# A fused attention and MLP block: inputs loaded on two queues, segment 0 projected in token halves, and a new instruction list

## The chip, the cores and the metric

The kernel runs on one core of one Trainium2 chip. The metric is device microseconds of one execution; the lower the better. The engines are PE (matrix multiply), ACT (ScalarE), DVE (VectorE), POOL (GpSimd) and SP (SyncE, which here only issues transfers). PE writes its results to eight banks of PSUM, from which ACT and DVE read.

## What is computed

The reference has two parts, each with a residual, on one sequence of 2048 tokens of width 640 in bf16.

```
h  = x + A(layernorm(x))          # attention with a memory, 32 heads of 20, 4 segments of 512 tokens
h2 = h + B(layernorm(h))          # silu(x @ w1) @ w2, with 1728 hidden columns

# A, for segment s of each head, phi(t) = t+1 where t>0, else exp(t):
p     = softmax(q_s k_s^T * 20**-0.5, causal)
a_dot = p v_s
a_mem = (phi(q_s) M) / (phi(q_s) z + 1e-6)
o     = g * a_mem + (1-g) * a_dot          # g = sigmoid(beta) per head
M    += phi(k_s)^T v_s ;  z += sum phi(k_s)
# then o @ wo
```

In segment 0 the memory is empty, so only softmax attention is left there.

## The kernel before, in words

The program is a list of named tasks. Each task is declared with the engines it may run on, what it reads and writes, and its buffers from pools; the order in which tasks are emitted, the engine of a task that may run on several, and the slot of every buffer are written out by hand in `ORDER` (L359). An entry such as `qe010y/A:0` would mean: this task, on ACT (D is DVE, G is POOL, S is SP), slot 0. Each engine takes its own tasks strictly in that order; a tracker (L43) adds the semaphore waits, so a task that waits holds up everything behind it on its engine. Transfers are entries of the list too and take a place on the queue of the engine that issues them.

Tasks of a segment s, with the lines of their instructions:

- `x0`, `x4` and so on load tokens, 128 to a block (L567); `w_q`, `w_k`, `w_wv`, `w_wo`, `w_w1_*`, `w_w2_*` load weights (L570). wq and wk land in raw form in the space of `sT` and are copied (`re_wq0` to `re_wk4`, L682 on ACT, L684 on DVE) into `wqr` and `wkr`, where four heads stand 32 rows apart and the 12 rows between take parts of other heads.
- layer norm: `n1_st` (L711, L714 on DVE), `n1_ra` and `n1_rb` (L720 and L725 on POOL: variance plus epsilon, then the power -0.5), `n1_ap` (L732). In segment 0 the result is transposed by PE (`n1_tp`, L741) and copied out by ACT (`n1_te`, L750); later by a transposing transfer (`n1_tr`, L756).
- `v` (L783) and its copy `ve` (L793, L794); the projections of Q and K `pr` (L817), five chunks c each, and their copies `qe` (L825 on ACT, L826 on DVE) into `QK`. `vt` (L857, twelve transfers of SP) gathers the parts of other heads from `QK` into `QKV`, so that 32 heads make eight groups of four: five in `QK`, three in `QKV`.
- the memory's features `ex` (L832), `pha` (L839), `phb` (L845), and M's update `kt`, `mz`, `ma`, `mb` (L1050 to L1094).
- per group, scores `qk` (L893), which fill four PSUM banks at once; their exps `e` (two of 1024 columns, L904 on ACT); the causal mask `mk` (L915 on POOL); the product with V, `av` (L936); its scaled copy `oe` (L949 on ACT, L951 on DVE); a transposing matmul with the memory's share, `tn` (L965, L969); the normalisation `nm` and `ad` (L982 to L1010). There are 168 exps. In segment 0 each group comes in two halves of queries: `x` (the first 256 tokens, 384 columns of scores per head) and `y`.
- `ot`, `wo`, `rs` (L1111 to L1127): output projection and residual; layer norm again; `h1` (L1153, 13 blocks of 128 hidden columns, and L1148, the tail of 64 columns, two tiles of 64 side by side in the array), `th` (tanh on ACT, L1162), `s` (L1168 on DVE), `h2` (L1195), `o` (L1208) and the store `out` (L1213). In segment 0 h1 is done in two halves of the tokens.
- `fill` (L604) are matmuls on zeros, put in by the list where PE would have nothing to do.

The tasks of segment s+1's projections, segment s's attention and segment s-1's MLP are interleaved in the list. At the end only PE's MLP work of the last segments is left.

At the start, x0, x1, wv, wq, wk, beta and the rest are issued by SP in that order, x2 and x3 by ACT. `QK`, `QKV`, `xT` and `hT` exist once each. All other transfers are SP's.

Of the kernel before, what the change touches and what calls it, by code (L numbers as in the profile page):

```python
# [6 lines left out]
ALU = mybir.AluOpType  # L7
# [340 lines left out]
SPLIT0 = ()  # L348
# [10 lines left out]
zpad:0 vpad0 iota x3:4 x1:3 x0:7 x2:5 sel w_wv:0 warm:0 vpad1 w_q:0 w_k halfc epsc beta x4:0,1,2,6 n1_st0:1 w_wo:0  # L359
w_w2_4 n1_st1:6 n1_ra0 w_w1_0:0 n1_rb0 n1_ap0:0 n1_ra1 n1_st2:2 fill30:0 n1_tp0:4 n1_rb1 n1_te0/A:0 n1_st3:0 n1_ra2  # L360
epsg0 n1_rb2 fill8:1 v00:0 mt1 n1_ap2:1 n1_ra3 n1_ap1:0 n1_rb3 n1_tp1:2 n1_tp2:6 mt2 n1_ap3:2 n1_te1/A re_wq1/D:0
n1_tp3:4 n1_te2/A re_wq4/D v01:2 ve00/D:1 n1_te3/A re_wq2/A pr010:6 re_wk0/A:0 re_wk1/D ve01/D pr011:7 qe010/D:0
re_wk3/D re_wk4/A lsc0 lsc1 re_wq0/D pr001:0 re_wk2/D qe011/A qk1x0:4 qe001/D:0 pr000:1 e1x2:5 n1_st6:0 e1x0 pr021:0
re_wq3/D qe000/A n1_ra6 mk1x_0 lsc2 n1_st7:4 ex001:0 qk0x0:4 n1_rb6 pr020:2 e0x2:0 mt3 mk1x_256 qe021/D:0 e0x0 lsc3
pr041:3 n1_st5:5 qe020/A vt00:0 n1_st4:7 qk2x0:4 n1_ra5 qe041/A:0 mk0x_0 pr031:1 zf0 vt09 vt06 e2x2:2 n1_rb5 mk0x_256
pr030:0 e2x0 n1_ap5:2 pha041:1 x8:8,9,10,11 qe031/A:0 mk2x_0 vt03 qk0yb0:4 qe030/D av1x:3 e0yb0:1 pr040:2 mk2x_256
n1_ra7 pha001:0 e0yb2 oe1x/D:0 av0x:3 qe040/D mk0yb_0 qk1yb0:4 oe0x/A:1 av2x:0 e1yb0:3 tn1x:1 v03:2 pha021:2 nm1x:3,0
e1yb2 mk0yb_256 phb001 n1_ap6:1 oe2x/A:0 mk1yb_0 qk3x0:4 ve03/D v02:0 n1_tr5:0 vt011 vt07 e3x2:4 vt04 n1_rb7 n1_st9:1
e3x0 ex021:2 ve02/D vt05 vt010 qk4x0:4 mk3x_0 n1_ra4 tn0x:2 e4x0:6 nm0x:0 vt01 mk3x_256 e4x2 n1_st8:6 fill7:3 qk0ya0:0
mta1 vt02 av3x:4 e0ya0:5 mk4x_0 vt08 oe3x/D:1 n1_st10:0 mk4x_256 e0ya2 fill6:5 qk1ya0:4 n1_tr6 v11:0 n1_rb4 e1ya0:0  # L370
n1_st11:3 n1_ra10 mta3 kt00:1 n1_ra8 e1ya2 av4x:2 ve11/D:0 tn2x:3 n1_ra11 phb021 qk5x0:4 n1_ap4:3 fill10:0 v12:0 e5x2:2
n1_ap7:1 n1_tr4 oe4x/D:0 e5x0 nm2x:1 ex011:2 n1_tr7 ve12/D qk6x0:4 mk5x_0 tn4x:2 e6x0:4 av0y:3 nm4x:0 mk5x_256 tn3x:0
e6x2 oe0y/D:0 kt02:0 n1_rb11 av5x:1 ex041:1 n1_ap11:3 qk7x0:4 mk6x_0 v10:2 nm3x:1 w_w2_5 e7x2:6 oe5x/D:1 mta2 mtb3 e7x0
mk6x_256 w_w1_1 w_w1_4 ve10/D qk2ya0:4 mk7x_0 v13:0 e2ya2:5 n1_ra9 mk7x_256 mk1yb_256 e2ya0 tn0y:2 av7x:3 ve13/D n1_rb8
oe7x/A:0 qk2yb0:4 nm0y:1 tn7x:0 e2yb0:1 av6x:1 nm7x:2 tn5x:2 av1y:3 e2yb2 oe6x/D:1 nm5x:3 tn6x:0 oe1y/A:0 qk3ya0:4
mk2yb_0 nm6x:0 e3ya0:2 n1_rb10 ot1:0 mk2yb_256 pha011:0 phb011 e3ya2 tn1y:2 pr101:1 mz02:0 qe101/D:0 av2y:3 ot0 ma02/A:3
qk3yb0:4 oe2y/D:1 mz00:1 e3yb2:0 phb041 pr100:3 ma00/D:0 kt01:1 nm1y:1 e3yb0 tn2y:2 zf1 qe100/D qk4ya0:4 mk3yb_0 kt04:0
wo1:0 e4ya0:6 nm2y:2 mk3yb_256 mtb1 e4ya2 w_w2_2 av3y:3 rs1 w_w1_3 ex031:0 qk4yb0:4 oe3y/D:0 w_w1_2 wo0:0 e4yb2:5
n2_st1:5 w_w2_1 e4yb0 epsg1 tn3y:2 ex101:1 n2_ra1 rs0 mm5 qk5ya0:4 pr140:3 n2_rb1 mk4yb_0 n2_st0:2 e5ya2:0 e5ya0 pr121:0
n2_ap1:0 n2_ra0 nm3y:0 qe140/A:0 mt0 n2_rb0 n2_tr1:0 qk5yb0:4 pr141:1 mta0 e5yb2:3 n2_ap0:2 mk4yb_256 n2_tr0 e5yb0 mtb0  # L380
pha031:1 phb031 av4y:2 mm6 qk6ya0:4 mm4 qe121/D:0 ex140:2 mk5yb_0 pr111:3 e6ya2:6 mk5yb_256 e6ya0 pr120:0 qe111/D:0
qe141/D ex121:0 qk6yb0:4 pha101:2 av5y:3 e6yb0:4 oe4y/D:0 h1_0_7_0:1 qe120/D e6yb2 h1_0_0_0:2 oe5y/D:1 th0_7_0:1 mk6yb_0
# [78 lines left out]
def build(nc, es, A_x, A_wq, A_wk, A_wv, A_wo, A_beta, B_x, B_w1, B_w2, out):  # L461
# [102 lines left out]
    def load_x(b0, n, prio, bw=2.1, kind="plain", engs=(SP,)):  # L564
        s0 = b0 % 12
        dma(f"x{b0}", [], [(X[b], [0]) for b in range(b0, b0 + n)],
            lambda e: e.dma_start(out=x_tok[:, s0:s0 + n, :], in_=xv[:, b0:b0 + n, :]), prio, bw, kind, engs=engs)  # L567
# [701 lines left out]
```

## Time and profile before

| | |
|---|---|
| median of 3 runs | 305.44 us (304.98 to 305.56) |
| the profiled execution: span from its first to its last instruction | 303.6 us |
| median less that span | 1.84 us |
| busy time of PE, ACT, DVE, POOL | 294.4, 226.6, 214.4, 141.7 us |
| first V matmul, first exp, start of the last exps | 9.03, 16.72, 240.89 us |
| end of the last matmul | 301.3 us |
| ACT busy in 16.7 to 37.7, 37.7 to 191, 191 to 242 us | 19.49, 142.74, 42.58 us |
| granted PE clock in every slice | 1.0 of full |

The profiler's own time of an execution is its span; the median includes what lies around it, and the table gives the difference. A line of a timeline reads: start, duration of the group, engine, line of the kernel, operation, output and input tile, shape, number of instructions, and in square brackets the idle time before it and who ended it. The line's duration runs from the first start to the last end; matmuls are pipelined, so that the next group starts before that end. A line of the table by stage gives the busy time of each engine in it with its instructions in parentheses, then the granted PE clock, the share of the 16 DMA engines that was busy, and the GB/s moved.

### The profile page before, as it was taken

The numbers are of one execution on the slowest core, as the hardware profiler recorded it, in microseconds if no ns is written. First come the engines' busy times: TensorE is split into PE (matmuls) and PEld (weight loads), VectorE is DVE, ScalarE is ACT, GpSimd is POOL, SyncE is SP. The second block draws the span as 40 slices with busy tenths as digits, with TensorE's granted clock in tenths as the row PEclk, the third lists the DMA queues.
The fourth block names the chain that finished last, engine by engine and source line by source line (L and its number), as shares of the span: only waits on it lengthen the run. The fifth ranks groups of instructions, "written<-read, shape, count | busy, mean of one in ns | idle before, by whom it ended". The sixth has DMA issues, their size and how long they took to land.

```text
span 303.6 us, 7334 instructions
## 1 busy us (share of the span) xinstructions
PE 294.4 (97%) x2934; PEld 167.9 (55%) x2934; DVE 214.4 (71%) x492; ACT 226.6 (75%) x321; POOL 141.7 (47%) x280
## 2 busy tenths in 40 slices
PE   6999989999999999999999999999999999999996
PEld 5634545466565455566643545556564466764565
DVE  4888967877868866958588975858847494835623
ACT  3689988999999999899889989968779951004500
POOL 3346574532875856546847317564564730400000
PEclk9999999999999999999999999999999999999999
DMA  6938375843544130063551300043241006221003
GB/s 211 363 104 159 69 153 87 272 37 77 166 87 75 39 42 2 2 122 69 106 154 42 67 19 0 2 89 69 56 97 36 2 0 89 43 66 66 0 3 107
DMA packets 48721, 24.65 MB, mean 81 GB/s; under 512 B 39152, under 2 KB 47600, under 8 KB 48688
## 3 DMA queue, kind: packets, MB, share of 16 engines
q1 hardware_dynamic: 48400, 23.86, 34.6%
q8 instruction: 23, 0.38, 0.5%
q10 hardware_dynamic: 288, 0.33, 0.4%
q14 instruction: 10, 0.08, 0.1%
HBM read 10.41 MB, written 2.62 MB: 43 GB/s over the span
## 4 chain that ended last, share of the span: by engine, by line
PE 72%; ACT 12%; DVE 7%; DMA 4%; SPq 2%; issue 1%; POOL 0%; ACTq 0%
PE ps_all L1195 17%; PE ps_all L1153 13%; PE ps_all L817 13%; ACT PT L904 8%; PE ps_all L893 7%; PE ps_all L1119 6%; PE ps_all L783 5%; PE ps_all L936 5%; DVE sT L1168 3%; DMA wv_sb<-in_A_wv_dram 2%; ACT th L1162 2%; PE ps_all L965 2%; PE ps_all L1058 2%; DMA x_tok<-in_A_x_dram 1%; PE ps_all L969 1%
## 5 line engine op out<-in xcount | busy, mean ns | idle before, releaser
L904 ACT ACTIVATE PT<-ps_all 128x1024 bf16<-128x1024 f32 (+1 forms) x168 | 156.3, 985 | 16.9 <-PE ps_all L893 15.9
L915 POOL TENSOR_SCALAR_AFFINE_SELECT PT<-PT 128x512 bf16<-128x512 bf16 x128 | 81.5, 650 | 52.8 <-ACT PT L904 51.5
L1195 PE MATMUL ps_all<-w_sb,sT 128*128 128x320 bf16 (+2 forms) x462 | 64.8, 295 | 0.1
L1153 PE MATMUL ps_all<-hT,w_sb 128*128 128x512 bf16 (+1 forms) x325 | 62.5, 337 | 0.5 <-DVE sT L1168 0.4
L1162 ACT ACTIVATE th<-ps_all 128x512 f32<-128x512 f32 (+2 forms) x70 | 34.0, 505 | 35.1 <-PE ps_all L1153 24.6
L1168 DVE SCALAR_TENSOR_TENSOR sT<-th,ps_all 128x512 bf16<-128x512 f32 (+2 forms) x70 | 37.6, 558 | 23.8 <-ACT th L1162 23.2
L1195 PEld LDWEIGHTS ps_all<-w_sb,sT 128*128 128x128 bf16 x462 | 43.2, 98 | 18.5 <-issue 1.9
L1153 PEld LDWEIGHTS ps_all<-hT,w_sb 128*128 128x128 bf16 x325 | 29.8, 98 | 25.4 <-issue 2.1
L1010 POOL TENSOR_TENSOR otok<-on 128x320 bf16<-128x320 bf16 x24 | 19.2, 804 | 23.7 <-DVE on L1002 23.6
L711 DVE BATCH_NORM_STATS2 stt<-x_tok 128x6 f32<-128x320 bf16 x64 | 27.8, 476 | 3.4 <-DMA x_tok<-in_A_x_dram 3.2
L1208 DVE SCALAR_TENSOR_TENSOR x_tok<-ps_all,x_tok 128x640 bf16<-128x640 f32 (+3 forms) x18 | 13.3, 748 | 19.0 <-PE ps_all L1195 18.9
L720 POOL TENSOR_TENSOR rst<-mvt,eps_c 128x1 f32<-128x1 f32 x32 | 7.1, 223 | 40.4 <-DVE mvt L714 36.0
L817 PE MATMUL ps_all<-xT,wqr 128*128 128x512 bf16 x100 | 25.0, 381 | 0.0
L783 PE MATMUL ps_all<-wv_sb,xT 128*128 128x320 bf16 x160 | 24.4, 300 | 0.4 <-DMA wv_sb<-in_A_wv_dram 0.3
L817 PE MATMUL ps_all<-xT,wkr 128*128 128x512 bf16 x100 | 24.8, 380 | 0.0
L1119 PE MATMUL ps_all<-wo_sb,oT 128*128 128x320 bf16 x160 | 24.1, 299 | 0.4 <-DVE rd L996 0.2
L936 PE MATMUL ps_all<-PT,Vx 128*32 128x256 bf16 (+3 forms) x576 | 24.4, 287 | 0.0
L893 PE MATMUL ps_all<-QK 20*128 20x256 bf16 (+3 forms) x360 | 20.5, 286 | 1.0 <-ACT PT L904 0.7
L1002 DVE TENSOR_TENSOR on<-ps_all,rd 128x640 bf16<-128x640 f32 x24 | 19.8, 824 | 1.9 <-POOL otok L1010 1.1
L826 DVE CAST QK<-ps_all 128x512 bf16<-128x512 f32 x25 | 16.9, 684 | 5.1 <-PE ps_all L817 5.0
L1119 PEld LDWEIGHTS ps_all<-wo_sb,oT 128*128 128x128 bf16 x160 | 14.8, 97 | 8.1 <-issue 2.8
L783 PEld LDWEIGHTS ps_all<-wv_sb,xT 128*128 128x128 bf16 x160 | 14.7, 98 | 7.9 <-issue 1.5
(71 smaller groups left out, 329.4 us busy)
## 6 DMA issues: line engine op xcount, KB each, us to landing
out_dram<-x_tok SPq DMA_DIRECT2D x15, 160.0 KB, 1.9
w_sb<-in_B_w_dram SPq DMA_DIRECT2D x5, 432.0 KB, 4.5
x_tok<-in_A_x_dram SPq DMA_DIRECT2D x3, 640.0 KB, 5.3
w_sb<-in_B_w_dram SPq DMA_DIRECT2D x3, 480.0 KB, 3.8
QKV<-QK SPq DMA_DIRECT2D x16, 72.0 KB
wv_sb<-in_A_wv_dram SPq DMA_DIRECT2D x1, 800.0 KB, 7.2
sT<-in_A_wq_dram SPq DMA_DIRECT2D x1, 800.0 KB, 8.9
sT<-in_A_wk_dram SPq DMA_DIRECT2D x1, 800.0 KB, 10.6
```

The costliest lines, as they stand in the source:

```text
L711: T.add(DV, lambda e, hh=hh: e.bn_stats(out=stt[:, s, 6 * hh:6 * hh + 6], in_=xb[:, 320 * hh:320 * hh + 320]), reads=R((xa, xsub)), writes ...
L783: fns.append(lambda e, c=c, hh=hh: e.matmul(bank(ps, hh)[:, 0:320], lhsT=xT[:, c, 128 * i:128 * i + 128], rhs=wv_sb[:, c, 320 * hh:320 * h ...
L817: fns = [lambda e, kc=kc: e.matmul(bank(ps)[:, lo:hi], lhsT=wt[:, kc, c, :], rhs=xT[:, kc, lo:hi], start=(kc == 0), stop=(kc == NC - 1)) f ...
L893: fns.append(lambda e, j=j, o=o, r=r, q0=q0, q1=q1, qa=qa, ka=ka: e.matmul(ps_all[:, o:o + q1 - q0], lhsT=ka[32 * r:32 * r + DH, 128 * j:1 ...
L904: T.add(AC, lambda e: e.activation(out=pt[:, pta.slot, q0:q0 + 2, 0:width], in_=sc3[:, b0:b0 + 2, 0:width], func=ACT.Exp, scale=SCALE), re ...
L915: T.add(PO, lambda e: e.affine_select(out=v, in_=v, pattern=[[0, 4], [1, 128]], compare_op=ALU.is_ge, fill=0.0, base=0, channel_multiplier ...
L936: fns.append(lambda e, j=j, r=r, h=h, pa=pa, pt=pt, co=co, q0=q0, ji=ji: e.matmul(bank(po)[32 * r:32 * r + 32, q0:hi], lhsT=Vx[:, vx.slot, ...
L1119: fns.append(lambda e, c=c, hh=hh: e.matmul(bank(ps, hh)[:, 0:320], lhsT=oT[:, c, 128 * i:128 * i + 128], rhs=wo_sb[:, c, 320 * hh:320 * h ...
L1153: fns = [lambda e, c=c: e.matmul(bank(ps)[:, lo:hi], lhsT=w1_sb[:, c, 128 * f:128 * f + 128], rhs=hT[:, c, lo:hi], start=(c == 0), stop=(c ...
L1162: T.add(AC, lambda e: e.activation(out=th[:, tha.slot, lo:hi], in_=bank(ps)[:, lo:hi], func=ACT.Tanh, scale=0.5), reads=R((ps, [0])), writ ...
L1168: T.add(DV, lambda e: e.scalar_tensor_tensor(out=sT[:, f, lo:hi], in0=th[:, tha.slot, lo:hi], scalar=1.0, in1=bank(ps)[:, lo:hi], op0=ALU. ...
L1195: fns.append(lambda e, f=f, t0=t0, fr=fr, hh=hh, n=n: e.matmul(bank(pa, hh)[:, 0:n], lhsT=sT[:, f, t0:t0 + 128], rhs=w2_sb[:, fr, c0 + 320 ...
```

## The change

- The first loads: SP issues x0, wq, wv's first three fifths, beta, x4, wo and w1; ACT issues x1, x2, x3, wk, the rest of wv, and x8.
- Segment 0's projections of Q and K are done in halves of 256 tokens (`pr..x`, `pr..y`): 20 groups of five 256-column matmuls for ten of five 512-column ones. The first scores need only the first half. V is projected after them.
- Segment 0's Q and K stand in the space of w2 (`QZ`, `QZV`) and its transposed x in `hT`; `QK`, `QKV` and `xT` are left to the later segments. w2's four large loads therefore wait for the scores of segment 0.
- Tasks may be issued elsewhere: `vt`, w2's loads, `x8` and the stores by SP or ACT; the addition of epsilon by DVE or POOL. By the new list ACT issues 22 transfers (2 before): five at the very start, x8, eight `vt`, two w2 loads and six stores. 15 of the 20 half copies of segment 0's Q and K are on ACT.
- The tail of h1 is computed in four tiles of 32 columns by 128 or 256 tokens each, for two of 64: 20 matmuls for ten.
- `ORDER` is new as a whole. It holds one `fill` (37 matmuls, at the start); before there were 61 in five places.

Instruction counts of the two programs, where they differ: PE 2936 and 3012 (matmuls of projections, tails and fill); on ACT 512-column copies of Q and K 15 and 5, 256-column ones 0 and 15, copies of V 5 and 10, `oe` of 512 columns 13 and 9, of 256 columns 4 and 2, rearranging copies of wq and wk 7 and 2; DVE takes what ACT lost and the reverse. `th`, `ex` and the exps are the same in number.

The core of the diff:

```diff
-SPLIT0 = ()
+SPLIT0 = tuple((c, w) for c in range(5) for w in range(2))
...
+    w2_flat = w2_sb[:, :, :].rearrange("p f e -> p (f e)")
+    QZ = w2_flat[:, 0:10 * L].rearrange("p (c w t) -> p c w t", c=5, w=2)
+    QZV = w2_flat[:, 10 * L:16 * L].rearrange("p (c w t) -> p c w t", c=3, w=2)
...
-    load_x(1, 1, -99, 2.33, "fix", (SP,))
-    load_w("wv", wv_sb[:, :, :], cw(A_wv), -98, 4.96, [(W["wv"], [0])], "fix", (SP,))
+    load_x(1, 1, -100, 2.33, "fix", (AC,))
...
+    load_w("q", wraw[:, 0, :, :], cw(A_wq), -99, 6.58, [(sT0, ["q"])], "fix", (SP,))
+    load_w("k", wraw[:, 1, :, :], cw(A_wk), -99, 8.51, [(sT0, ["k"])], "fix", (AC,))
+    load_w("wv0", wv_sb[:, 0:3, :], cw(A_wv[0:384, :]), -95, 4.96, [(W["wv"], [0])], "fix", (SP,))
+    load_w("wv1", wv_sb[:, 3:5, :], cw(A_wv[384:640, :]), -95, 4.96, [(W["wv"], [1])], "fix", (AC,))
...
+    def load_w2():
+        qk, va = segs[0]["qk"], (segs[0]["qv"], list(range(12)))
+        WA = {0: [(qk[0], WH), (qk[1], WH), (qk[2], WH[:2])], 1: [(qk[2], WH[2:]), (qk[3], WH), (qk[4], WH[:2])],
+              2: [(qk[4], WH), va], 3: [va]}
+        for k, (f0, f1) in enumerate(((0, 4), (4, 7), (7, 10), (10, 13))):
+            load_w(f"w2_{k}", w2_sb[:, f0:f1, :], cw(B_w2[128 * f0:128 * f1, :]), 2 + k, 0.45 * (f1 - f0),
+                   [(W["w2"], [k])] + WA[k], engs=(SP, AC))
...
+            if eng == DV:
+                T.add(DV, lambda e: e.tensor_scalar(out=rst[:, s, :], in0=mvt[:, s, 1:2], scalar1=EPS, scalar2=None,
+                                                    op0=ALU.add), reads=R((st, ["mv"])), writes=R((st, ["r"])))
...
-        xTa = G.alloc("xT")
+        xTa = G.alloc("xT" if s else "hT")
+        xT_ = xT if s else hT
...
+        QK_, QKV_ = (QZ, QZV) if s == 0 else (QK, QKV)
...
-            dma(f"vt{s}{n}", reads, [(qv, [n])], lambda e: e.dma_start(out=o, in_=i_), pr, 0.25, "sb", lane=lane_v[n % 3 > 0])
+            dma(f"vt{s}{n}", reads, [(qv, [n])], lambda e: e.dma_start(out=o, in_=i_), pr, 0.25, "sb", lane=lane_v[n % 3 > 0], engs=(SP, AC))
...
-                            bank(ps)[64 * k:64 * k + 64, lo:hi], lhsT=w1_sb[:, c, 128 * f:FF],
-                            rhs=hv[:, c, k, b0 // 2:b1 // 2, :], start=(c == 0), stop=(c == NC - 1),
-                            tile_position=(0, 64 * k)) for c in range(NC) for k in range(2)]
+                            bank(ps)[32 * k:32 * k + 32, lo:hi],
+                            lhsT=w1_sb[:, c, 128 * f + 32 * (k % 2):128 * f + 32 * (k % 2) + 32],
+                            rhs=hv[:, c, k // 2, b0 // 2:b1 // 2, :], start=(c == 0), stop=(c == NC - 1),
+                            tile_position=(0, 32 * k)) for c in range(NC) for k in range(4)]
...
-                    pr, 0.6, lane=lane_o)
+                    pr, 0.6, lane=lane_o, engs=(SP, AC))
```

The start of the new list, up to the first exps:

```
epsc:0 zpad mt0 iota vpad0 sel x1:3 n1_st1:6 mta0 mtb0 mm6 mm4 mt2 mm2 x0:7 x2:5 mta2 x3:4 mtb2 epsg0 mm7 mt1 mt3
w_k:0 w_wv1:0 n1_st0:1 n1_st2:2 halfc n1_r1/G n1_ap1:1 n1_r0/G n1_ap0:0 w_q mta3 n1_r2/G mm9 mtb3 n1_st3:0 w_wv0 beta
x4:0,1,2,6 re_wq2/D:0 re_wq0/D n1_ap2:3 warm:0 w_wo:0 mm11 mm8 w_w2_4 x8/A:8,9,10,11 re_wk0/D:0 w_w1_0:0 w_w1_3
n1_r3/G mta1 mm0 w_w1_1 re_wk2/D n1_ap3:2 re_wq1/D re_wk3/D re_wq3/D mtb1 mm1 fill37:0 mm3 w_w1_2 vpad1 w_w1_4 mm5
mm10 w_w2_5 n1_tp1:1 n1_te1/A:0 n1_tp0:6 n1_te0/A pr020x:5 re_wk1/A qe020x/A:0 pr000x:6 qe000x/A:0 n1_tp2:3 n1_te2/A
pr001x:2 qe001x/A pr011x:6 qe011x/A:0 zf0 re_wk4/D zf1 lsc0 lsc1 mzc4 mzc8 mzc11 mzc6 mzc5 mzc10 lsc2 re_wq4/D
n1_st4:7 mzc7 mzc9 n1_r4/G mzc3 mzc1 mzc2 mzc0 epsg1 n1_st7:4 n1_st6:5 n1_r6/G n1_r7/G n1_tp3:0 n1_te3/A pr010x:3
qe010x/A qk0x0:4 e0x2:0 e0x0
```

## The prediction

> **What bounds the kernel now.** I read the busy line first, then the chain of work that ended last, then the timelines of PE and ACT in the middle of the run.
>
> ```profile
> PE 294.4 (97%) x2934; PEld 167.9 (55%) x2934; DVE 214.4 (71%) x492; ACT 226.6 (75%) x321; POOL 141.7 (47%) x280
> ...
> PE 72%; ACT 12%; DVE 7%; DMA 4%; SPq 2%; issue 1%; POOL 0%; ACTq 0%
> ```
>
> A busy PE need not be a full one, so I compare starts with starts:
>
> ```profile
> 114.74 1.24 PE L817 MATMUL ps_all<-xT,wkr 128*128 128x512 bf16 x5
> 115.82 0.71 PE L1153 MATMUL ps_all<-hT,w_sb 128*128 128x256 bf16 x5
> 116.50 0.40 PE L893 MATMUL ps_all<-QKV 20*128 20x512 bf16 x4
> 116.83 1.25 PE L817 MATMUL ps_all<-xT,wkr 128*128 128x512 bf16 x5
> ```
>
> Each group starts before the one ahead has ended: five 512-column matmuls take 1.08 us start to start, a score group of four 0.33. Between them there is no hole, and from 45 us to the end I found none above 0.5. So PE is the bound. ACT comes next: by the busy times by stage it works 142.7 of the 153.3 us from 37.7 to 191. PE is idle 9.2 us in all (303.6 less 294.4): 1.1 before its first instruction, 1.2 and 0.35 before 9.03, 2.3 after its last one (301.3 to 303.6), and 4.2 elsewhere. Beside that stand filler matmuls on zeros: 38 before 9.03, and 23 later (some 2.6 us at 0.11 each). Useful work starts at 9.03 but for one transpose. That is all there is to win: about 8.6 us at the start, 6.8 in the middle.
>
> **Part 1, the loads and the start.** What must land before the first scores changes: x, wq and wk now go ahead of wv, on two queues. Before, by stage:
>
> ```profile
> 3.00:4.00 1.00, 1.00 (x7) 0.73 (x5) 0.00 (x0) 1.00 (x1) 0.00 (x0) 1.00 1.07 387
> 4.00:5.00 1.00, 1.00 (x9) 0.81 (x8) 0.22 (x1) 0.26 (x1) 0.00 (x0) 1.00 0.68 224
> ...
> 9.00:10.00 1.00, 0.97 (x8) 0.73 (x9) 0.96 (x4) 0.00 (x0) 0.86 (x4) 1.00 1.06 389
> ```
>
> The last column is GB/s: 387 while SP and ACT both have a queue filled, 224 to 323 from 4 to 8 us with SP alone, 350 to 390 from 8 us, still SP alone. wk landed at 2.79 + 10.6 = 13.4 us, when 3.70 MB had moved, though 3.04 MB stood in front of its end: landing lags by some 0.65 MB. In the new order wk ends as the fifth transfer of ACT's queue (1.28 MB); with an equal share for SP's that is 2.56 MB, with the lag 3.2. At 380 from 3 us on (0.26 MB moved by then) wk lands at 10.75; at the rates of before 12.0; with half the lag 9.9. I take 10.75, since the row with two queues is the 387.
>
> [...]
>
> From wk on: the rearranging copies on ACT (0.53 + 0.40, less overlap) end at 11.7. ACT then has, in its new order, four half evacuations and one more before the first exp (128x256 reads: 0.39 by the th row, 0.31 start to start), two transposed blocks (0.70 each, 0.6) and two small exps (0.22): 11.7 + 1.55 + 1.2 + 0.3 = 14.75, say 14.85. PE's pieces in between (0.55 per half projection, 0.33 scores) end earlier; its holes there are some 1.3 us, and after the hole of 1.2 before 7.36 the granted clock stayed at 1.0. x8, which ACT now issues before its first transposed block, meets an ACT that waits anyway. Before it was
>
> ```profile
> 16.72 1.51 ACT L904 ACTIVATE PT<-ps_all 128x768 bf16<-128x768 f32 x2 [0.77 <-PE ps_all L893]
> ```
>
> So ACT starts its exps 1.9 us sooner (1.2 later or 0.9 sooner at the ends). But what counts is PE. In segment 0, 15 half evacuations on ACT replace five whole ones. Counting by mean durations, ACT does 23.75 us between the starts of exp 1 and exp 19 (36 instructions, each overlapping the next by 0.08: 20.9), against 19.5 before, of which 1.5 idle. Exp 19 starts at 35.7 instead of 36.22. PE has done the same by then in both: 20 transposing matmuls (1.2), 5 V blocks (7.1), the projections (11.0; as 20 halves at 0.56, 11.2), 10 score groups (3.3), 4 or 5 AV groups (1.4), 24.2 us in all. So the start is worth **-0.5 us** (-1.5 to +0.8), halves included. Doing projections before wv costs PE what the sooner exps bring: before, V matmuls filled 9.03 to 13.
>
> **Part 2, w2's space for segment 0's Q and K, hT for its x.** No instruction is added; w2's four loads now wait for the scores of segment 0, two of them on ACT, ahead of exps whose scores PE computes after the ones waited for, so those waits are met when ACT comes to them. The last is issued soon after the scores of segment 0 end (63 us before), lands 3.8 us later by the issues' list, and h2 first needs it at 81: some 10 us of cover, and I cost it at nothing. Were it late, PE, which takes its groups in order, would stand still for as long. The gain, that segment 1's projections need not wait for QK, has no wait in the trace of before to remove: 0.
>
> **Part 3, copies moved between ACT and DVE.** From exp 19 to the last, ACT has 5.0 us less to do (203.6 against 208.6 by counts times mean rows: fewer QK and oTs evacuations, more Vx). PE waits in that stretch are 3.5 us in all, and 1.1 of filler; the ones I see are mostly of scores for ACT. ACT is not the bound there, so I take a quarter, **-1.2** (0 to -3.5). DVE gains some 5 us on 214 and nine additions to the variance; it has 89 us idle: 0.
>
> **Part 4, the tail of h1 in four tiles of 32 instead of two of 64.** Five tails; columns per tile are the same, matmuls double to 20.
>
> ```profile
> 192.79 0.74 PE L1148 MATMUL ps_all<-hT,w_sb 128*64 128x256 bf16 x10
> 193.46 0.39 PE L893 MATMUL ps_all<-QK 20*128 20x512 bf16 x4
> ...
> 39.13 0.57 PE L936 MATMUL ps_all<-PT,Vx 128*32 128x256 bf16 x16
> 39.66 0.25 PE L969 MATMUL ps_all<-ident,oTs 128*128 128x84 bf16 x2
> ```
>
> A whole tail takes 0.67 now, a half one 0.40 (123.70 to 124.10). The nearest row with 32-wide tiles is AV: 16 matmuls in 0.53, 33 ns each however few their columns. 20 make 0.68: 2 x 0.28 + 3 x 0.02 to 0.07, **+0.8** (0 to 1.4).
>
> **Part 5, transfers issued by ACT amid its work.** Between its first and its last exp ACT now issues eleven: eight of the virtual-head copies, two w2 loads, one store. Before it issued none there, only two at the start:
>
> ```profile
> 0.80 0.87 ACTq L567 DMA_DIRECT2D x_tok<-in_A_x_dram  x2
> 1.70 1.28 ACT L585 ACT_TABLE_LOAD   x1 [1.70 <-PEq L1254]
> ...
> L857 SPq DMA_DIRECT2D QKV<-QK x12: 624/682/897, 21.3 to 32.2; - x12
> ```
>
> Each issue holds its queue: 0.43 there, and the table load begins only after them; 0.68 for a virtual-head copy on SP. Upper end: all of it delays the exps queued behind: 8 x 0.68 + 2 x 0.5 + 0.43 = 6.9 us, and PE, whose next scores need the PSUM banks that these exps read, waits with them. Lower end 0: ACT's rows overlap (two exps of 1.02 in 1.94), so the queue runs ahead of the engine. No row shows an issue behind a running exp; the nearest is the one above, with nothing in front. I take 0.25 each, nearer to hidden because an exp lasts 1.0 and the issue 0.7: **+2.75**. On SP nothing waits that the chain shows (2%), so relief there is 0.
>
> **Part 6, the new list's end.** PE work left after the last scores is 59.0 us of columns against 58.5, and h1 of segment 3 alternates its two th buffers somewhat better (before, 19 us for 14.6 of columns, with h2 matmuls filling most): 0.
>
> **Sum**: -0.5 - 1.2 + 0.8 + 2.75 = +1.85. The profiled span is 303.6; 1.84 us of the 305.44 median lie around it and stay. 303.6 + 1.84 + 1.85 = **307.3 us**.
>
> **Rivals.**
> - *Hidden issues, ACT relief in full* (faster). If the issues cost nothing, and PE's 3.5 us of waits and half of its 1.1 us of filler go: -0.5 - 4.0 + 0.8 = -3.7, rounded against late waits to -2.8: 302.6; with wk at 9.9, 301.7. For it: ACT's overlapping rows and its 5 us less. Against: PE's waits are few already, and some are for DVE. [...]
> - *Full price of the issues* (slower still): -0.5 + 0.8 + 6.9 = +7.2, 312.6. It decides from 0.1 us per issue on: there eleven issues outweigh the -0.9 of the other terms.
> - *No change*: the terms cancel at about 0.1 us per issue: 305.4.
> - *The change does not do what it says*: wk lands no sooner (12.0 us): 308.5, inside the range.
>
> **How the numbers follow.** Forecast (306.1 to 310) 0.43, full price 0.18, hidden 0.31, no change 0.08. The low end is 301.7, the high end 312.6. A measurement of this kernel tells about 0.2% (0.6 us) from no change. Faster 0.31, same 0.08, slower 0.61.
>
> **What would show it.** First exp at 14 to 16 us and exp 19 near 35.7 (part 1); L1148's successor starting 0.68 us after a tail; ACT's idle before an exp just behind an ACTq row of 0.25 (part 5; near 0 makes the hidden rival, 0.6 the full price); PE idle plus filler between 36 us and 240 us above 4.6 us. I would be wrong if PE's waits fall below 2 us there, or if the first exp comes after 17 us.

## The result, and the profile after

The changed kernel takes 309.48 us (median of four runs, 307.8 to 310.2) against 305.21 before (304.25 to 305.56): a ratio of 1.0137, 95% interval 1.0102 to 1.0172, some 4.2 us slower. One run of experiment 4 and one of the kernel before, with a mean granted clock of 0.69 and 0.85, are left out of all comparisons. The forecast was 307.3. The profiled run took 309.25 us, its span is 307.5 (before 303.6), and its last PE instruction ends at 305.03 (before 301.29): the 3.74 us to explain.

The page of the changed kernel, busy shares and chain:

```profile
PE 293.9 (96%) x3010; PEld 171.8 (56%) x3010; DVE 221.8 (72%) x513; ACT 224.4 (73%) x319; POOL 141.3 (46%) x271
...
PE 74%; ACT 9%; DVE 7%; DMA 6%; issue 1%; ACTq 1%; SPq 1%; DVEq 0%
```

PE is still the bound, but DMA has gone from 4 to 6% of the chain: by lines, wk's load holds 3% and the transposes of the attention output (oT) 2%. The busy line says nothing of what was lost, so I compared the starts of the same exps in both traces: exp 1 at 17.78 (before 16.72), exp 19 at 39.05 (36.22), exp 97 at 136.8 (135.0), exp 168 at 245.47 (241.81). So 2.83 us are lost by exp 19, 1.03 are won back by exp 97, 1.86 are lost behind it, and 0.08 after the last. Exp 19, before and then in the changed kernel:

```profile
36.22 1.51 ACT L904 ACTIVATE PT<-ps_all 128x768 bf16<-128x768 f32 x2 [0.54 <-PE ps_all L893]
```

```profile
39.05 1.51 ACT L925 ACTIVATE PT<-ps_all 128x768 bf16<-128x768 f32 x2
```

**The start.** ACT's timeline, then PE's, then the stages (the last three columns are the granted clock, the DMA share and GB/s):

```profile
13.02 0.83 ACT L692 ACTIVATE wkr<-sT 128x400 bf16<-128x400 bf16 x2 [3.48 <-DMA sT<-in_A_wk_dram]
...
17.78 1.51 ACT L925 ACTIVATE PT<-ps_all 128x768 bf16<-128x768 f32 x2
```

```profile
7.75 0.81 PE L759 MATMUL ps_all<-ident,xn_rot 128*128 128x128 bf16 x10 [1.13 <-DVE xn_rot L750]
10.00 1.71 PE L837 MATMUL ps_all<-hT,wqr 128*128 128x256 bf16 x10 [1.44 <-DVE wqr L694]
...
13.50 2.32 PE L837 MATMUL ps_all<-hT,wkr 128*128 128x256 bf16 x10 [1.25 <-DVE wkr L694]
```

```profile
8.00:10.00 2.00, 0.56 (x10) 0.35 (x7) 1.58 (x8) 1.30 (x2) 1.62 (x7) 1.00 0.60 175
...
12.00:14.00 2.00, 0.75 (x6) 0.39 (x4) 0.98 (x5) 0.98 (x3) 0.67 (x4) 0.50 1.07 377
14.00:16.00 2.00, 2.00 (x13) 1.45 (x12) 1.65 (x12) 1.41 (x5) 0.00 (x0) 0.50 1.07 364
```

wk lands at 13.0 us; ACT and PE wait for it. Between 6.6 and 13.5 PE has three holes above a microsecond, and from 10.6 to 17.5 us the granted clock is 0.50: the ten matmuls at 13.50 take 2.1 us start to start, at full clock 1.09 (experiment 10). By links, exp 19's delay of 2.83 is -0.36 (ACT's rearranging of wk begins at 13.02, before at 13.38), +1.42 (from there to exp 1: 4.76 against 3.34), +1.77 (exp 1 to exp 19: 21.27 against 19.50).

**The wait at 139.** PE, and SP's queue ahead of it:

```profile
141.06 1.53 PE L1140 MATMUL ps_all<-wo_sb,oT 128*128 128x320 bf16 x10 [1.90 <-DMA oT<-otok]
```

```profile
130.53 2.55 SPq L1132 DMA_TRANSPOSE oT<-otok  x2
134.41 1.33 SPq L877 DMA_DIRECT2D QKV<-QK  x2
135.78 3.58 SPq L1132 DMA_TRANSPOSE oT<-otok  x2
```

All four blocks' data were there by 130.5 (POOL's last addition to otok starts at 129.71 and takes 0.79). But SP takes its list in order: two transposes, then a virtual-head copy that waits for a projection until 134.4, and the other two transposes behind it. In the trace of before no hole of PE from 105 us on is above 0.4.

### The profile page after: what moved, and what is told of

It reads as the page before. It is cut to its first block, busy times and chain, and to the rows that moved or that the text cites. A ratio compares the mean times of both kernels' runs of the same rounds, so it can differ in the third digit from the quotient of the medians.

```text
span 307.5 us, 7509 instructions
## 1 busy us (share of the span) xinstructions
PE 293.9 (96%) x3010; PEld 171.8 (56%) x3010; DVE 221.8 (72%) x513; ACT 224.4 (73%) x319; POOL 141.3 (46%) x271
## 3 DMA queue, kind: packets, MB, share of 16 engines
HBM read 10.41 MB, written 2.62 MB: 42 GB/s over the span
## 4 chain that ended last, share of the span: by engine, by line
PE 74%; ACT 9%; DVE 7%; DMA 6%; issue 1%; ACTq 1%; SPq 1%; DVEq 0%
PE ps_all L1217 20%; PE ps_all L1175 15%; PE ps_all L837 11%; ACT PT L925 7%; PE ps_all L914 7%; PE ps_all L1140 6%; PE ps_all L957 5%; PE ps_all L802 5%; DMA sT<-in_A_wk_dram 3%; PE ps_all L986 2%; DMA oT<-otok 2%; PE ps_all L1079 1%; PE ps_all L990 1%; DMA w_sb<-w_sb 1%; DVE stt L728 1%; DVE oTs L972 1%
## 5 line engine op out<-in xcount | busy, mean ns | idle before, releaser
L925 ACT ACTIVATE PT<-ps_all 128x1024 bf16<-128x1024 f32 (+1 forms) x168 | 157.0, 986 | 14.4 <-PE ps_all L914 12.5
L936 POOL TENSOR_SCALAR_AFFINE_SELECT PT<-PT 128x512 bf16<-128x512 bf16 x128 | 82.6, 651 | 78.3 <-ACT PT L925 75.1
L1175 PE MATMUL ps_all<-hT,w_sb 128*128 128x512 bf16 (+1 forms) x325 | 63.2, 337 | 0.0
L1184 ACT ACTIVATE th<-ps_all 128x512 f32<-128x512 f32 (+2 forms) x70 | 34.6, 508 | 37.8 <-PE ps_all L1169 19.5
L1190 DVE SCALAR_TENSOR_TENSOR sT<-th,ps_all 128x512 bf16<-128x512 f32 (+2 forms) x70 | 38.4, 562 | 20.0 <-ACT th L1184 19.4
L957 PE MATMUL ps_all<-PT,Vx 128*32 128x256 bf16 (+3 forms) x576 | 23.5, 287 | 1.2 <-DVE rd L1003 0.8
L744 POOL TENSOR_TENSOR rst<-rst,eps_c 128x1 f32<-128x1 f32 x32 | 18.5, 577 | 11.4 <-DVE rst L738 9.6
L972 DVE TENSOR_SCALAR oTs<-ps_all,lsc 128x512 bf16<-128x512 f32 (+1 forms) x29 | 17.7, 617 | 4.8 <-PE ps_all L957 4.5
L750 DVE TENSOR_SCALAR xn_rot<-x_tok,mvt,rst 128x640 bf16<-128x640 bf16 x32 | 15.7, 498 | 5.2 <-POOL rst L744 5.2
L837 PE MATMUL ps_all<-xT,wqr 128*128 128x512 bf16 x75 | 18.7, 380 | 0.3 <-ACT PT L925 0.3
L837 PE MATMUL ps_all<-xT,wkr 128*128 128x512 bf16 x75 | 18.7, 380 | 0.1
L957 PEld LDWEIGHTS ps_all<-PT,Vx 128*32 128x32 bf16 x576 | 12.4, 96 | 10.8 <-issue 3.5
```

The lines of the kernel that those rows point to most:

```text
L837: fns = [lambda e, kc=kc: e.matmul(bank(ps)[:, lo:hi], lhsT=wt[:, kc, c, :], rhs=xT_[:, kc, lo:hi], start=(kc == 0), stop=(kc == NC - 1)) ...
L925: T.add(AC, lambda e: e.activation(out=pt[:, pta.slot, q0:q0 + 2, 0:width], in_=sc3[:, b0:b0 + 2, 0:width], func=ACT.Exp, scale=SCALE), re ...
L936: T.add(PO, lambda e: e.affine_select(out=v, in_=v, pattern=[[0, 4], [1, 128]], compare_op=ALU.is_ge, fill=0.0, base=0, channel_multiplier ...
L957: fns.append(lambda e, j=j, r=r, h=h, pa=pa, pt=pt, co=co, q0=q0, ji=ji: e.matmul(bank(po)[32 * r:32 * r + 32, q0:hi], lhsT=Vx[:, vx.slot, ...
L972: f = lambda e: e.tensor_scalar(out=o, in0=i_, scalar1=lsc[:, g:g + 1], scalar2=None, op0=ALU.mult)
L1175: fns = [lambda e, c=c: e.matmul(bank(ps)[:, lo:hi], lhsT=w1_sb[:, c, 128 * f:128 * f + 128], rhs=hT[:, c, lo:hi], start=(c == 0), stop=(c ...
```

## The experiments

Each experiment runs the changed kernel with the edit shown, but for the last but one. Ratios are to the kernel before on the same chip.

**1. Fillers in the start's holes.**

```diff
- fill37:0
+ fill44:0
- n1_tp0:6 n1_te0/A pr020x:5 ... n1_tp2:3 n1_te2/A pr001x:2
+ n1_tp0:6 n1_te0/A fill11:0 pr020x:5 ... fill4:0 n1_tp2:3 n1_te2/A fill11:0 pr001x:2
```

> The changed kernel with 33 more matmuls on zeros at the start (37 becomes 44, and 11, 4 and 11 in the three waits of PE between 8.5 and 13.5 us); no other instruction moves, and the waits for wq and wk stay as long as they were. Theory A (the start costs two things: PE waits, and in them the granted clock falls to 0.50 until 18 us, which makes 25 projection matmuls take 4.8 us in place of 2.75): the clock stays near 1.0, PE saves about 2, the first exp comes near 16 us in place of 17.8, and the time is 307.3 to 308 in place of 309.5. Theory B (the slow matmuls stand under the wait for wk and for ACT, so that the clock costs nothing): the clock is back at 1.0 and the time stays at 309.5 +-0.4. If the clock stays low even so, it doesn't hang on PE's holes.

307.15 us, 1.0069 (1.0043 to 1.0094); clock 1.00 through the profiled run. The time fits theory A, the trace does not: exp 1 is at 17.72. ACT met wk at 14.16 there, 1.1 later, and from wk to exp 1 it took 3.56 in place of 4.76. So the clock is worth 1.2 us behind wk, and the rest of the gain in this trace is the wait at 139, which did not come (the same two transposes, issued at 135.69, landed some 2 us sooner). The four traces with this order of transposes have the wait at 1.90 (the change), 2.19 (experiment 2), 0.82 (3) and nothing (1). So it differs from run to run, and both causes had to be taken apart.

**2. wk second on ACT's queue.**

```diff
- x1 ... x2 ... x3 ... w_k w_wv1      (ACT's queue; n1_st2 and n1_st3 right behind n1_st0)
+ x1 ... w_k x2 ... x3 ... w_wv1      (n1_st2, n1_st3, n1_ap2 behind re_wk0; n1_tp2 behind pr011x)
```

> The changed kernel with wk as the second transfer of ACT's queue, ahead of x2 and x3; the statistics and the transposes of blocks 2 and 3 go behind the first rearranging copies and the first four half projections. Theory A (wk's landing at 13.0 us, not the half projections, is why the first exp came 1.1 us later than before): 0.98 MB of ACT's queue end with wk in place of 1.31, so it lands at 8.5 to 11, PE's wait of 1.3 at 13.5 goes, the first exp comes at 14.5 to 16, and the time is 306.5 to 308. Theory B (what the queue gives first is paid back: x2 and x3 now land after 11 us, their transposes and the copies on ACT wait, and exp 7 comes no sooner than 24.5): 309 to 310.

311.26 us, 1.0199 (1.0177 to 1.0221). wk landed at 9.68, and it is slower than theory B even: ACT and PE stood waiting for blocks 2 and 3.

```profile
14.26 0.45 PE L759 MATMUL ps_all<-ident,xn_rot 128*128 128x128 bf16 x5 [2.42 <-DVE xn_rot L750]
```

In PE's list the transposes of blocks 2 and 3 stand ahead of the first scores, which need only blocks 0 and 1. Exp 1 came at 17.40, and the clock was 0.50 from 15.9 to 19.3 us and again from 43.2 to 46.6.

**3. ACT's transfers back on SP.**

```diff
- vt07/A vt011/A vt03/A vt15/A ... w_w2_0/A w_w2_2/A ... out6/A ...
+ vt07/S vt011/S vt03/S vt15/S ... w_w2_0/S w_w2_2/S ... out6/S ...
```

> The changed kernel with the 16 transfers that ACT issues behind its first exp (eight copies for the virtual heads, two loads of w2, six stores) issued by SP, in the same places of the list. Theory A (the issues lie under running exps, since ACT's sequencer takes them while its engine works): the time stays within 0.5 of 309.5, or grows by the waits that SP's longer queue makes for the transposes behind it. Theory B (the prediction's part 5, 0.25 us each for eleven of them): 306.7, 2.75 less. At the full 0.6 each it would be 303.

310.50 us, 1.0189 (1.0153 to 1.0225): not faster, theory A. From exp 19 to exp 168, where eight of the eleven issues lie, it takes 205.36 us, in the changed kernel 206.43; less each one's oT wait (0.82 and 1.90) that is 204.54 and 204.53. Eight issues at 0.25 would have made 2.0. The change's own trace shows why:

```profile
24.47 0.81 ACT L925 ACTIVATE PT<-ps_all 128x768 bf16<-128x768 f32 x1
24.55 1.49 ACTq L877 DMA_DIRECT2D w_sb<-w_sb  x1
25.17 0.81 ACT L925 ACTIVATE PT<-ps_all 128x768 bf16<-128x768 f32 x1
26.09 0.66 ACT L845 ACTIVATE w_sb<-ps_all 128x256 bf16<-128x256 f32 x2
```

An issue of 1.49 us (24.55 to 26.04) runs beside two exps: the one of 25.17 starts in the middle of the issue, and ACT is idle 0.11 behind it. Whether a longer issue would lie under exps as well, no run here shows. On the other side, SP alone needed 8.91 us for the twelve copies of segment 0 (23.69 to 32.6) where SP with ACT needed 6.79 (24.55 to 31.3), and PE then waited 1.81 for them at 34.86 (0.47 in the changed kernel); behind that wait the granted clock was 0.50 from 36.3 to 39.8.

**4. The two oT transposes ahead of the copies.**

```diff
- ot7 pha240:0 ... qe230/D vt210/S ... vt24/S ... ot4 mk16e_0 mk16e_256 ot5 ex240:2
+ ot7 ot4 ot5 pha240:0 ... qe230/D vt210/S ... vt24/S ... mk16e_0 mk16e_256 ex240:2
```

> The changed kernel with one move on SP's queue: the transposes of blocks 4 and 5 of the attention output go ahead of two copies for segment 2's virtual heads, which wait for a projection. Theory A (PE's wait of 1.9 us at 139 is SP's order: the copy waits to 134.4 and both transposes, whose data are there by 130.5, stand behind it): they are issued by 133, land by 136, the wait goes, and the time is 307.5 to 308. Theory B (PE runs into the next thing that is late, scores for ACT or the copies that now come 2.5 us later): 309 to 309.7.

307.96 us, 1.0080 (1.0053 to 1.0108): theory A by the time. The trace of this kernel is that of experiment 9.

**5. Experiments 1 and 4 together.**

> Both edits that gained, together: the 33 more fillers of fill_holes and the two transposes ahead of ot_ahead. In fill_holes' trace the first exp came when it did before (17.72, with wk landing 1.1 later, at 14.16), and the wait of 1.9 us at 139 was missing, so its 2.3 us may be partly that wait. Theory A (the two are separate, the half clock costs 1.2: first exp 4.76 us behind wk in the changed kernel, 3.56 with fillers): 306.4 to 307.1, that is 309.5 less 1.2 less 1.5. Theory B (the sums of the medians hold, 2.3 and 1.5): 305.7. Theory C (fillers do nothing but that the wait at 139 happened not to come): 308.0, as ot_ahead.

306.65 us, 1.0051 (1.0033 to 1.0069): theory A. wk at 12.52, exp 1 at 16.07 (3.55 later), clock 1.00, no wait at 139. It is the base of the next three and of experiment 10.

**6. beta behind x4.**

```diff
- w_wv0 beta x4:0,1,2,6
+ w_wv0 x4:0,1,2,6 beta       (its readers zf0, lsc0 and so on behind the third exp)
```

> ot_fill with the broadcast of beta (128 rows of 64 bytes) behind x4 on SP's queue instead of ahead of it, and what reads beta behind the third exp. Theory A (the hole in the transfers from 8 to 10 us, 212 and 138 GB/s in the changed kernel with 124 packets under 512 B, is beta's packets, which the other queue's wk shares engines with): the hole moves to 12 to 15 us, wk lands about 1.2 us sooner (11.8 to 12.8), the first exp comes as much sooner, and the time is 1 to 1.3 below ot_fill. Theory B (the hole is not beta's): wk lands as in ot_fill, and so does the time, +-0.3.

307.34 us, 1.0085 (1.0064 to 1.0106). Half of each theory. The stage from 9 to 10 us, first of the changed kernel, then of this one:

```profile
9.00:10.00 1.00, 0.00 (x1) 0.03 (x1) 0.96 (x6) 0.54 (x1) 0.69 (x4) 1.00 0.50 138
```

```profile
9.00:10.00 1.00, 1.00 (x11) 0.77 (x8) 0.99 (x5) 0.99 (x2) 0.90 (x4) 1.00 1.07 361
```

So the hole is beta's: it moved with beta (259 and 294 GB/s from 12 to 14 us). But wk landed at 12.5 as in experiment 5. The traces by queue show most of the reason: from 8 to 10 us SP's queue moved 0.35 MB in place of 0.13, and ACT's, on which wk stands, 0.37 in place of 0.31. Beta had held up above all the queue that it stands on. The 0.7 us lost are a new wait of PE for DVE, 1.33 at 28.5: beta's small operations now stand in the middle of DVE's list and wait there for POOL, 0.92 at 23.9, so that the copy that PE needs comes at 27.96 (26.56 in experiment 5).

**7. The tail of h1 as two tiles of 64.** The edit puts the old lines of the diff back.

> ot_fill with the tail of h1 as before the change: two tiles of 64 columns, 10 matmuls, in place of four of 32, 20 matmuls; the rest is the same. Theory A (a 32-wide matmul takes no longer per tile, since four run beside each other: in the changed kernel the half tail gives way after 0.39 us, before 0.40): +-0.3 from ot_fill, and the whole tail's successor starts as late in both. Theory B (the prediction's part 4, 33 ns each): 0.8 below ot_fill.

306.71 us, 1.0058 (1.0040 to 1.0076) against 1.0051: theory A. The changed kernel's half tail and what follows it, then a whole tail:

```profile
133.91 0.46 PE L1169 MATMUL ps_all<-hT,w_sb 128*32 128x128 bf16 x20
134.30 1.53 PE L1140 MATMUL ps_all<-wo_sb,oT 128*128 128x320 bf16 x10
...
202.36 0.73 PE L1169 MATMUL ps_all<-hT,w_sb 128*32 128x256 bf16 x20
203.02 0.40 PE L914 MATMUL ps_all<-QK 20*128 20x384 bf16 x8
```

The whole tail takes 0.66 us, as 0.67 for ten matmuls before: 33 ns each, the pace of AV's row. The half tail takes 0.39, as 0.40 before: 20 ns each. So 33 ns is the pace at 256 columns, not a floor for 32-wide tiles.

**8. The first half's scores ahead of blocks 2 and 3.** Experiment 5 with wk second as in 2, with 23 fillers more than the change in place of 33, and

```diff
- n1_tp2:3 n1_te2/A pr001x:2 ... n1_tp3:0 n1_te3/A pr010x:3 qe010x/A qk0x0:4 e0x2:0 e0x0
+ pr010x:3 ... pr001x:2 ... pr011x:1 qk0x0:4 e0x2:0 e0x0 pr021x:0 qk1x0:4 e1x2:1 e1x0 n1_tp2:2 n1_te2/A qk2x0:4 ...
```

> ot_fill with wk second on ACT's queue as in wk_second, and with PE's and ACT's lists changed so that nothing of blocks 2 and 3 stands ahead of the first half's scores: six half projections and the scores and exps of heads' groups 0 and 1 go ahead of the transposes of blocks 2 and 3. Theory A (the first exp is tied to wk, and from there to exp 19 ACT is the bound at 21.3 us): wk lands near 9.7, first exp at 12 to 13.5, exp 19 at 33.5 to 36.2 against 38.95, and the time is 2.5 to 4 below ot_fill, that is below the kernel before. Theory B (ACT runs dry behind the first groups, since blocks 2 and 3 and the other half's projections come later, or PE, the bound from 40 us on, has no less to do and gives nothing back): exp 19 at 37 or later, or the time within 1 of ot_fill.

310.37 us, 1.0181 (1.0162 to 1.0200): theory B. Exp 1 came at 14.26, the earliest of all, exp 7 at 26.95 (22.71 in experiment 5) and exp 19 at 41.91. PE and ACT there:

```profile
19.31 1.25 PE L837 MATMUL ps_all<-hT,wqr 128*128 128x256 bf16 x5 [0.80 <-ACT hT L768]
20.35 1.27 PE L837 MATMUL ps_all<-hT,wkr 128*128 128x256 bf16 x5
```

```profile
21.66 0.39 ACT L845 ACTIVATE w_sb<-ps_all 128x256 bf16<-128x256 f32 x1 [2.41 <-PE ps_all L837]
```

PE had waited 0.97, 1.23 and 0.80 for ACT, the clock was 0.50 from 19.3 to 22.7 us, five matmuls took 1.05, and my list had put an evacuation ahead of group 2's exps, whose scores had been ready at 18.1.

**9. Experiment 4 again.**

> The kernel of ot_ahead once more, beside the next one on the same chip and for a trace of its own. If fillers are worth the difference between ot_ahead (307.96) and ot_fill (306.65), it comes out 1 to 1.3 above ot_fill's ratio to before, 1.0075 to 1.009; its trace shows no wait of PE at 139 to 141, a granted clock of 0.5 from about 12 to 17 us, and some 4.7 us from wk's landing to the first exp.

307.24 us, 1.0077 (1.0055 to 1.0100): both within what was expected, and no wait at 139:

```profile
130.53 5.20 SPq L1132 DMA_TRANSPOSE oT<-otok  x4
```

```profile
139.10 1.53 PE L1140 MATMUL ps_all<-wo_sb,oT 128*128 128x320 bf16 x10
```

But the half clock was not at 12 us, though PE waited 1.11 and 1.81 there; it came at 41:

```profile
38.00:40.00 2.00, 1.23 (x24) 0.57 (x28) 1.82 (x8) 2.00 (x4) 1.17 (x3) 1.00 0.34 74
...
42.00:44.00 2.00, 2.00 (x10) 1.09 (x8) 0.53 (x2) 1.88 (x2) 0.34 (x1) 0.50 0.03 6
```

From exp 19 to exp 25 it takes 7.58 us there, 6.04 in experiment 5. From wk to exp 1 it takes 3.55, as with fillers, where 4.7 had been expected: the 1.2 us of the changed kernel belong to the half clock in that stretch.

**10. wk on SP's queue, wv on ACT's.** Experiment 5 with

```diff
-    load_w("k", ..., [(sT0, ["k"])], "fix", (AC,))
-    load_w("wv0", ..., [(W["wv"], [0])], "fix", (SP,))
+    load_w("k", ..., [(sT0, ["k"])], "fix", (SP,))
+    load_w("wv0", ..., [(W["wv"], [0])], "fix", (AC,))
```

> ot_fill with wk moved from ACT's queue to SP's, right behind wq, and both parts of wv to ACT's queue in its place (the 11 fillers ahead of K's first projection become 4). In every trace so far SP's queue moved 0.55 to 0.60 MB from 4 to 6 us and ACT's 0.14 to 0.18. Theory A (ACT's queue is served late at the start, and wk's place on it sets the first exp): 1.80 MB of SP's queue end with wk, which by the rates of ot_fill without beta (1.0 MB at 6 us, 0.2 per us then) is 10 to 11 us in place of 12.5; first exp 14 to 15 in place of 16.1, exp 19 at 35 to 36, and 304.3 to 305.6. Theory B (PE, DVE and ACT are each full from 16 to 37 us, and PE sets the end: an earlier start is given back as waits of PE, as in x_half_first): 306 to 307.

306.19 us, 1.0030 (1.0015 to 1.0045). wk landed at 11.06 and exp 1 came at 15.23, sooner, nearly as theory A has it; exp 19 came at 37.68, later than in experiment 5 (37.29), and the time is theory B's. DVE waited 1.49 for x4, which had moved back, and PE's idle time from 20 to 40 us grew from 1.90 to 2.95. The shares of the queues in the changed kernel from 4 to 6 us (q1 is SP's, q10 ACT's):

```profile
q1 hardware_dynamic: 460, 0.57, 82.8%
q10 hardware_dynamic: 139, 0.16, 22.4%
```

Both had several transfers outstanding, yet SP's moved 3.6 times as much; from 6 to 8 us it is 0.41 and 0.35 MB, from 12 to 14 us 0.38 and 0.37. So the two shares are near even in these later stretches and far apart in the first. Nor is the low share fixed: with wk second on ACT's queue (experiments 2 and 8) ACT's moved 0.26 and 0.32 MB from 4 to 6 us, SP's 0.47 and 0.45. What sets it, no run here takes apart.

**11. The kernel before without its 38 early fillers.**

```diff
- fill30:0 n1_tp0:4 ... fill8:1 v00:0
+ n1_tp0:4 ... v00:0
```

> The kernel before without its 38 matmuls on zeros ahead of 9 us (the 23 later ones stay). In 40 runs of the kernel before the mean granted clock is 1.00 (one apart), in the changed kernel's four 0.989, 0.989, 0.994 and 1.0, in those with 33 more fillers mostly 1.0 again. Theory A (the granted clock halves for some 4 us at a time after PE has stood idle or sparsely used in the first 15 us, and one such spell costs 1.0 to 1.5 us): without fillers the kernel before shows it too, mean clock 0.994 or lower in most runs, and takes 306.2 to 308. Theory B (the half clock belongs to the new lists, not to PE's idle time): clock 1.0 and 305.1 +-0.4.

307.25 us, 1.0069 (1.0053 to 1.0084), as theory A's time; but its sign did not come: the recorded mean clock is 1.00 in all six runs. The first V block (ten matmuls) takes 2.62 us start to start here, with fillers 1.36. Here, then in the kernel before:

```profile
9.10 2.83 PE L783 MATMUL ps_all<-wv_sb,xT 128*128 128x320 bf16 x10 [1.06 <-DMA wv_sb<-in_A_wv_dram]
11.72 1.70 PE L741 MATMUL ps_all<-ident,xn_rot 128*128 128x128 bf16 x15
```

```profile
9.03 1.52 PE L783 MATMUL ps_all<-wv_sb,xT 128*128 128x320 bf16 x10 [0.35 <-DMA wv_sb<-in_A_wv_dram]
10.39 1.17 PE L741 MATMUL ps_all<-ident,xn_rot 128*128 128x128 bf16 x15
```

And the stage here:

```profile
8.00:10.00 2.00, 0.94 (x5) 0.57 (x5) 1.93 (x7) 0.70 (x1) 1.46 (x6) 1.00 1.05 369
```

The clock's column does not show it, because the trace's clock record has its first entry only at 13.2 us in this run, and the column prints 1.00 ahead of that. In the kernel before the first entry stands at 4.4 us, and there the matmuls on zeros take 0.21 us each, start to start, up to 4.3 us and 0.11 behind. So in both kernels PE works at half pace ahead of the record, here still in the V block at 9.10 and the transposes behind it, and the mean clock does not count it. It is PE's idle time, then, as theory A has it, that costs here: 1.26 us in the V block alone (2.62 less 1.36). Exp 1 is 1.63 late and stays so (exp 19 at 37.85). A wait for oT of 0.92 at 134.9, which the trace of the kernel before does not have, comes on top.

**12. The best.** Experiment 10 with

```diff
-    load_x(4, 4, -90, engs=(SP,))        (behind beta)
+    load_x(4, 4, -90, engs=(AC,))        (ahead of wv0)
- n1_r10/G av5x:4
+ n1_r10/G fill4:5 av5x:4
```

> wk_on_sp with x4 (blocks 4 to 7) on ACT's queue ahead of both parts of wv instead of on SP's behind beta, and 4 fillers ahead of the AV group that waits 0.50 us at 38. In wk_on_sp DVE waited 1.5 us for x4 at 15.5 to 17.0, and exp 19 came at 37.7 though exp 1 came 0.8 sooner than in ot_fill; at 40 the clock halved. Theory A (x4 took back what wk had won): no wait of DVE at 15.5, exp 19 at 36 to 37, clock 1.0, and 304.6 to 305.6, that is level with the kernel before or below it. Theory B (from 16 us on PE, ACT and DVE are all full, so that an earlier start is lost by 40 us): 305.7 to 306.5.

305.26 us, 1.0009 (0.9993 to 1.0024): theory A, level with the kernel before, not below it. Exp 19 at 36.84, mean clock 0.999 or 1.00 in all twelve runs, no wait of DVE at 15.5.

## Why the prediction came out where it did, step by step

The direction held, and 309.5 lies inside the range around 307.3, but the loss was 4.2 us where 1.9 were forecast, and mostly not by the forecast's own terms: the term that carried the sum was nothing, and two losses that it did not have took its place. That the sum came as near as it did is luck. Two of its own signs told so: the first exp came at 17.78 (14 to 16 forecast, and the part wrong if after 17) and exp 19 at 39.05 (35.7).

- **Part 1, the start, -0.5: wrong, +2.83 in the profiled run.** The step that failed is "with an equal share for SP's": ACT's queue had a fifth of the traffic from 4 to 6 us, and wk on it landed at 12.5 to 14.2 us in every kernel with the change's order (10.75 forecast). On SP's it landed at 11.06 (experiment 10). That is +2.27 of the miss of 3.35. The rate of 380 GB/s held from 4 to 8 us (348 to 383) and failed behind that (212 and 138, beta), but without that hole wk still landed at 12.5 (experiment 6). The reading that SP's queue alone is slow from 4 to 8 us (224 to 323 GB/s) does not hold either: with the same transfers it moved 342 to 371 there in experiment 11. (The sizes 3.04, 1.28 and 2.56 MB take a KB of the issues' list as 1000 bytes; they are 3.11, 1.31 and 2.62, and as the lag shrinks with them, the 3.2 stays.) Next, "the granted clock stayed at 1.0": it did not, and of the 4.76 us from wk to exp 1 (4.1 forecast) 1.2 are the clock's. ACT's 20.9 from exp 1 to exp 19 was right to 0.4 (21.27), and so was its count: 36 instructions of 23.86 us, 27 of 20.34 before. The rival "wk lands no sooner" described the landing, and put too little on it.
- **The clock as a term: left out.** The mean granted clock is 0.999 or 1.00 in all 56 runs of the kernel before that the experiments' ratios use; with the new list and its 37 fillers (the change and experiments 2, 3, 4 and 9) it is 0.994 or lower in 24 of 26, with 26 to 33 more (1, 5, 6, 7, 10, 12) in 8 of 49, and in experiment 8, whose fillers left the later holes open, in 5 of 5. Runs of one kernel with 0.994 are 0.9 to 1.5 us longer than those with 1.00 in the kernels with more fillers (for instance 307.37 against a mean of 306.46 in experiment 5). That fillers prevent most spells of 0.50 is shown; what starts one is not, since experiment 9's came at 41 us behind a stage in which PE worked 1.23 of 2 us, while a hole of 1.81 at 12 us brought none. Why fillers ahead of 14 us should also keep off a spell near 40 is not shown either.
- **Part 2, w2's space, 0: right.** No wait of PE above 0.25 us stands in the changed kernel between 42 and 98 us, and h2 first needs w2 at 83.6.
- **Part 3, ACT's relief, -1.2: right in size.** From exp 19 to exp 168, less the oT wait, it takes 204.53 us against 205.59: -1.1. That is the sum of all parts of the change between these exps; parts 4 and 5 by themselves came to nothing.
- **Part 4, tails, +0.8: wrong, 0** (experiment 7). The step that failed is "33 ns each however few their columns": AV's row held groups of mostly 256 columns, and the half tail's 128 columns take 20 ns.
- **Part 5, ACT's issues, +2.75: wrong, 0** (experiment 3). The lower end was the truth, and the row it wanted is the one at 24.55. The rival of hidden issues was right on this and wrong on the time, because the start did not give what it too assumed.
- **SP's order, not seen.** A list with the transposes of blocks 6 and 7 first and a waiting copy ahead of 4 and 5 was in the new order to read; the prediction asked only whether SP is relieved.

Where the 4.2 us lie, by ratios: the order of the transposes, 1.0137 to 1.0079 (some 1.8 us); fillers, the half clock, to 1.0051 (0.8); wk and x4 behind the wrong transfers, to 1.0009 (1.3). By the intervals the first step is uncertain by 1.2 us and the other two by 0.7 to 0.8, so that the traces (1.90 us of wait, 1.2 us of half clock) carry more than the ratios do. What is left is within the interval. The last step carries four more fillers too and was not split. So the loss lies in the order of the queues and in the half clock, and with both repaired the change is level with the kernel before. It does not follow that no part of it is slow: from exp 1 to exp 19 even the best takes 21.55 us, 19.50 before, where ACT has more to do (36 instructions for 27, ten half copies of Q and K among them), and the sooner first exp and ACT's relief later on pay for that.

Why it is level and not faster is argued, not shown: from 16 to 37 us three engines are near full at once. Experiment 5, the stage from 20 to 24 us: PE 3.98, ACT 3.98 and DVE 3.14 of 4.00; 24 to 28: 4.00, 3.98 and 3.93. An earlier first exp would then be lost to whichever of them is next, and in experiments 2, 8 and 10 it was lost.

## What to carry to other kernels

When a transfer is moved to another queue, ask what its data waits for in that queue and what each consumer's list has ahead of it: the first weight to land is worth nothing if PE's list holds a block that lands later (experiment 2: wk at 9.68, exp 1 at 17.40). In a hand-ordered list, look at every instruction that waits on an in-order queue (SP's too) and read off what stands behind it; one such copy cost up to 1.9 us here. Price an issue between exps at nothing until a row shows a gap behind it (here 0.11 us behind an issue of 1.49; 204.53 us with eight issues on ACT and 204.54 without, experiment 3).

## What the runs showed of the hardware that was not expected

- The granted clock fell to 0.50 for some 3.4 us at a time (experiment 3, 36.3 to 39.8; experiment 8, 19.3 to 22.7; experiment 9, 41.2 to 44.6; twice in experiment 2, 15.9 to 19.3 and 43.2 to 46.6), and for 6.83 us on end in the changed kernel (10.64 to 17.46). The profiled runs with one stretch of 3.4 have a mean clock of 0.994, those with 6.8 in all 0.988 or 0.989. PE need not be idle throughout: it worked 1.23 of 2 us ahead of one (experiment 9, 38 to 40). The longest holes ahead of one here were 0.5 to 2.4 us. PE's busy share ahead of it does not decide it either: in experiment 9 a stretch that was 47% busy (10.5 to 13.9 us) brought none, and one that was 76% busy (37.8 to 41.2) did.
- PE started at half pace in the kernel before and in the changed kernel, up to the first entry of the clock record (4.4 and 3.81 us): 0.21 us per matmul on zeros ahead of it, 0.11 behind it, while the profile's clock reads 1.00 in both. Without the early fillers ten matmuls at 9.10 took 2.62 us against 1.36.
- A broadcast of 128 rows of 64 bytes held both queues together to 138 to 212 GB/s for two microseconds, where without it they moved 361 to 366; the queue that it stands on lost most (experiments 5 and 6: 0.13 MB in place of 0.35, the other's 0.31 in place of 0.37).
